# Converting four weight pieces during the first batch of attention, and dividing by the softmax sums with transferred rows on POOL

## The chip, the cores and the metric

The kernel runs on one core of a Trainium2 chip. The metric is the device time of one execution in microseconds (us); the time before is a median of 1040.71 us over three runs (1039.84 to 1042.85). Engines are named as in the profile: PE (matmul, PEld its weight loads), DVE (vector), ACT (scalar), POOL (GpSimd) and SP, whose only work here is to issue transfers.

## The reference

```python
q_bits = (einsum('bhsd,dk->bhsk', q, proj) > 0)          # 6 hash bits, also for k
mask   = bucket(q)[..., :, None] == bucket(k)[..., None, :]
scores = where(mask, q @ k.T / sqrt(64), -1e9)           # B, H, S, D = 4, 8, 768, 64
attn   = exp(scores - max); attn = attn / (attn.sum(-1) + 1e-9)
x      = (attn @ v).transpose(0, 2, 1, 3).reshape(3072, 512)
h      = x @ w_in                                         # 512 x 2048
out    = (h * clip(h + 3, 0, 6) / 6) @ w_out              # 2048 x 512
```

The weights come as 64-bit numbers. Products are made at nearly float32 accuracy: every operand is split into a high part and a low part, and three products (high-high, high-low, low-high) are summed.

## The kernel before

**Attention** is worked off in tiles of 128 keys by all 768 queries, six tiles to a head, eight heads to a batch. The iteration `k` of the main loop makes, in this order: the six transposes of tile k (`transp`, L337), the exponential of tile k+1 (L327, ACT), the minimum of tile k+2 (`lowest`, L315, DVE), half a value product (L374, L375), the split of tile k's transposed probabilities (L360 on ACT, L361 on DVE) and the scores of tile k+3 (L305, L308). Every sixth iteration (k divisible by six) also makes the hash products of the next head but some (`hash_qk`, L265 to L267) and turns them into bits (L276, DVE). POOL prepares queries and keys of a coming head once per head: `scale_q` (L232), the cast and two subtractions of `split_qk` (L253, L257, L258), `split_v` (L291, L292) and two accumulating transfers of outputs (L381). Copies of the cast halves (`kk<-qq`) go by SP's transfers and are needed by the hash products.

Tiles 0 to 47 are batch 0. Iterations 48 to 51 already belong to batch 1; at iteration 51 (`GB` = 52 tiles) attention pauses, and `first_ffn` works off the whole feed-forward part of batch 0: 16 column groups `fc` of the weights by three token chunks, 48 iterations of `gemm1` (L478 to L480), `gate` (L487 to L493) and `gemm2` (L500 to L502). Meanwhile the weights are **converted**: there are 32 pieces (two per `fc`, 128 x 512 each), and `convert` turns a raw 64-bit piece into its high and low part in steps: L175 and L177 on DVE, L182 on ACT, a minimum (L185 on POOL outside the feed-forward part, L188 on DVE inside it), L190 on DVE, L195 on ACT and L196 on POOL. Pieces 0 to 2 are converted beside iterations 45 to 51, the others inside `first_ffn`, a new one begun in two of three iterations (and in all three where `fc` is 4, 6, 8 or 10). Raw pieces and converted ones share one ring of 32 buffers; 28 raw pieces go through it, and the last four use output buffers. After `first_ffn` attention goes on beside the feed-forward part of batches 1 to 3, with all weights converted.

The attention output of batch 0 lies in DRAM undivided (`xs`). Six heads of it (the first three of four 128-row groups) are loaded in three chunks at iterations 40, 41 and 47 and **divided by the sums**: `inverse` (L418, L419), and for each chunk and group `spread` (L426, POOL: each inverse repeated 64 times along the free axis) and `normalise` (two PE transposes L436, then a DVE product L439 with the PSUM result). The first chunk is then split (L469, L470). The last two heads follow as `late`.

**What sets the order:** PE, DVE, ACT and POOL run their instructions in the order in which the code emits them (`manual_schedule`), and each waits in place for what an instruction needs. The table in `early` says which small steps are emitted at the end of which iteration. SP's transfers are put in order by a planner, and SP too waits in place.

Of the kernel before, what the change touches and what calls it, by code (L numbers as in the profile page):

```python
# [10 lines left out]
F32 = mybir.dt.float32  # L11
F32R = mybir.dt.float32r
# [6 lines left out]
P = 128  # L19
# [10 lines left out]
FB = 4  # L30
FS = 4
WL = 28
WE = 8
WA = 3
XE = 8
# [5 lines left out]
def lsh_attention_moe(  # L41
# [101 lines left out]
    def load_w(n: int):  # L143
        fc, k = divmod(n, 2)

        if n < WL:
            raw = cp.tile([P, 2 * WC], F32R, name=f"wr{n}", tag="w", bufs=NW)
        else:
            raw = sp.tile([P, 2 * WC], F32R, name=f"wr{n}", tag="ob")
# [50 lines left out]

    sms = {}


# [342 lines left out]
    room, late, conv, ready, rc0 = {}, {}, {}, {}, []  # L546
    flying = {2: 3}
    cc3 = NCC - 1

    def load0(t: int):  # L550
        xr0[t] = load_x(0, t, range(cc3))

# [19 lines left out]
    def early() -> dict[int, list]:  # L572

        todo = {n: [] for n in range(XE + FB + 1)}

        def put(n: int, *fs):
            todo[n] += fs

        def scaled(t: int):
            def items(x: int):  # L580
                if not sx[t]:
                    if not rc0:
                        rc0.append(inverse("0", 0, slice(0, S), range(cc3)))
                    sx[t].extend(scale_x(0, t, range(cc3), xr0[t], rc0[0][:, 2 * t : 2 * t + 2]))
                sx[t][x]()
            return [lambda x=x: items(x) for x in range(2 + cc3)]

        sx = {t: [] for t in range(NTC)}
        s0, s1, s2 = (scaled(t) for t in range(NTC))
        sp0 = [lambda cc=cc: split_x(x0[0][cc], xr0[0][:, cc], nc.gpsimd) for cc in range(cc3)]  # L590
        c0, c1, c2 = (lambda n=n: cv(n) for n in range(3))
        put(0, lambda: load0(0))
        put(1, lambda: load0(1))
        put(2, s0[0], s0[1], room0)
        put(3, s0[2])
        put(4, s0[3], sp0[0])
        put(5, s0[4], sp0[1], c0)
        put(6, sp0[2], s1[0], s1[1], c0)
        put(7, lambda: load0(2), s1[2], c0, c1)
        put(8, s1[3], c0, c1)  # L600
        put(9, s1[4], c0, c1, s2[0], s2[1], c2)
        put(10, s2[2], c1, c2)
        put(11, s2[3], c1, c2)

        put(12, s2[4])
        return todo
# [3 lines left out]
    def first_ffn(resume):  # L610
# [30 lines left out]
        for n, (fc, t) in enumerate(order):  # L641
# [27 lines left out]
            if n == 0:  # L669
                for f in early_steps[XE + FB]:  # L670
                    f()
# [4 lines left out]
            for x in at:  # L676
                stage[x] += 1
                if stage[x] == 6:
                    del stage[x]
                    if x >= WL and x + 2 < NW:  # L680
                        with tc.issue_after(last.ins):
                            load_w(x + 2)
                        ready[x + 2] = n + 2
            end = finish(*pend) if pend is not None else None
# [155 lines left out]
    with tc.manual_schedule(engines={ET.PE, ET.DVE, ET.Activation, ET.Pool}):  # L840
# [7 lines left out]
        for k in range(NS):  # L848
            end = GB if k < GB else NS
            i, t = divmod(k, KT)  # L850
            if k == HK - XE:
                lent += [cp.tile([P, 2 * WC], F32R, name=f"lent{n}", tag="w", bufs=NW) for n in range(2)]
            if k == GB:
# [40 lines left out]
            if k + LA >= NS:  # L894
                add()
            if HK - XE <= k < GB:
                for f in early_steps[k - HK + XE]:
                    f()
# [71 lines left out]
```

## Time and profile before

| what | value |
|---|---|
| median of three runs | 1040.71 us (1039.84 to 1042.85) |
| the profiled execution's own time | 1040.82 us |
| its span in the profile | 1039.0 us (1.8 us lie around it) |
| mean granted PE clock | 0.994 |
| busy: PE, DVE, ACT, POOL | 1009.5, 687.0, 583.6, 451.4 us |
| batch 0's attention, its last tiles, the first feed-forward part | up to 111, 111 to 147, 147 to about 297 us |

A view by stretches gives, for each stretch of the span, how long each engine was busy and what clock PE was granted. In a timeline a row has start, duration, engine, line, operation, and in brackets how long the engine idled before and what it waited for. In a view by groups a row ends with total busy time, mean duration in ns, and the idle time before the group.

### The profile page before, as it was taken

How to read it: one execution, taken by the hardware profiler on the slowest of the kernel's cores; microseconds unless marked ns; L12 is line 12 of the kernel's file. 1: busy time of each engine (PE TensorE's matmuls, PEld its weight loads, DVE VectorE, ACT ScalarE, POOL GpSimd, SP SyncE). 2: the span in 40 equal slices, each digit the busy share in tenths (PEclk: the TensorE clock that was granted, in tenths of full speed). 3: DMA queues.
4: the chain of work that ended last, by engine and by line, in shares of the span. 5: the costliest groups of instructions: out<-in, count | busy, mean ns of one | idle time of the engine just before them, and what ended most of it. 6: DMA issues, size and time to landing. Idle time of an engine off the chain costs nothing.

```text
span 1039.0 us, 18911 instructions
## 1 busy us (share of the span) xinstructions
PE 1009.5 (97%) x6846; PEld 927.2 (89%) x6846; DVE 687.0 (66%) x1441; ACT 583.6 (56%) x1308; POOL 451.4 (43%) x439
## 2 busy tenths in 40 slices
PE   8999879999999999999999999999999999999998
PEld 7999868887989998899999999999899999899997
DVE  6999888999479998766656666655665563333332
ACT  6888855555478887645554555454455462333332
POOL 5677753334247775645444444544454232200100
PEclk9999989999999999999999999999999999999999
DMA  3666686000144555322222232222232011101000
GB/s 93 155 149 155 187 277 236 1 2 1 46 130 112 120 124 143 80 53 60 75 46 63 61 88 59 53 71 59 60 93 47 15 37 28 42 1 41 1 22 20
DMA packets 47380, 80.68 MB, mean 78 GB/s; under 512 B 5892, under 2 KB 27780, under 8 KB 47288
## 3 DMA queue, kind: packets, MB, share of 16 engines
q1 hardware_dynamic: 42808, 73.98, 24.2%
q0 software_dynamic: 4480, 5.51, 4.6%
q8 instruction: 54, 0.88, 0.4%
q14 instruction: 38, 0.31, 0.1%
HBM read 41.95 MB, written 18.09 MB: 58 GB/s over the span
## 4 chain that ended last, share of the span: by engine, by line
PE 83%; DVE 8%; issue 3%; POOL 2%; ACT 2%; DMA 1%; SPq 0%; DVEq 0%; POOLq 0%; ACTq 0%
PE pt L337 11%; PE h L479 7%; PE h L478 7%; PE h L480 7%; PE po L500 7%; PE po L502 7%; PE po L501 7%; PE acc L374 6%; PE acc L375 6%; PE s L305 6%; PE s L308 6%; DVE wr L175 1%; DVE pl L361 1%; DVE wr L177 1%; PE z L267 1%
## 5 line engine op out<-in xcount | busy, mean ns | idle before, releaser
L315 DVE TENSOR_SCALAR_CACHE_REDUCE p<-s 128x768 f32<-128x768 f32 x192 | 183.5, 956 | 103.5 <-PE pt L337 99.5
L361 DVE TENSOR_TENSOR pl<-pt,ph 128x384 fp32r<-128x384 f32 x376 | 191.8, 551 | 50.4 <-ACT ph L360 48.3
L360 ACT CAST ph<-pt 128x384 fp32r<-128x384 f32 x376 | 165.5, 480 | 57.4 <-PE pt L337 45.0
L327 ACT ACTIVATE p<-p,m 128x768 f32<-128x768 f32 x192 | 179.5, 935 | 5.1 <-DVE p L315 4.8
L487 ACT ACTIVATE g<-h,three 128x256 f32<-128x256 f32 x192 | 91.4, 476 | 155.9 <-PE h L480 141.6
L337 PE MATMUL pt<-ident,p 128*128 128x128 f32 x1152 | 162.2, 275 | 5.9 <-DVE pl L361 4.8
L493 POOL TENSOR_TENSOR gl<-g,gh 128x256 fp32r<-128x256 f32 x96 | 74.2, 773 | 203.7 <-DVE gh L492 160.0
L488 DVE SCALAR_TENSOR_TENSOR g<-g,h 128x256 f32<-128x256 f32 x192 | 80.6, 420 | 117.8 <-ACT g L487 115.3
L337 PEld LDWEIGHTS pt<-ident,p 128*128 128x128 f32 x1152 | 137.3, 141 | 23.6 <-PE pt L337 3.8
L374 PE MATMUL acc<-ph,vv 128*128 128x256 f32 x564 | 152.8, 303 | 1.0 <-DVE pl L361 1.0
L478 PE MATMUL h<-xh,w 128*128 128x256 f32 x512 | 147.7, 289 | 1.2 <-ACT y L402 1.2
L480 PE MATMUL h<-xh,w 128*128 128x256 f32 x512 | 143.4, 280 | 1.3 <-POOL w L196 1.3
L479 PE MATMUL h<-xl,w 128*128 128x256 f32 x512 | 143.2, 280 | 0.6 <-DVE xl L470 0.6
L375 PE MATMUL acc<-pl,vv 128*128 128x256 f32 x564 | 141.1, 283 | 0.0
L500 PE MATMUL po<-w,gh 128*128 128x512 f32 x320 | 126.7, 396 | 1.5 <-ACT gh L492 1.4
L501 PE MATMUL po<-w,gh 128*128 128x512 f32 x320 | 126.2, 394 | 0.9 <-POOL w L196 0.9
L502 PE MATMUL po<-w,gl 128*128 128x512 f32 x320 | 126.6, 396 | 0.0
L374 PEld LDWEIGHTS acc<-ph,vv 128*128 128x128 f32 x564 | 107.5, 191 | 2.2 <-DVE pl L361 1.9
L375 PEld LDWEIGHTS acc<-pl,vv 128*128 128x128 f32 x564 | 107.9, 191 | 0.0
L305 PE MATMUL s<-kk,qq 76*128 76x384 f32 x384 | 101.2, 344 | 2.5 <-ACT kk L281 1.5
L308 PE MATMUL s<-kk,qq 128*128 128x384 f32 x384 | 100.0, 341 | 0.0
L478 PEld LDWEIGHTS h<-xh,w 128*128 128x128 f32 x512 | 96.4, 188 | 3.8 <-ACT y L402 2.4
(134 smaller groups left out, 1999.5 us busy)
## 6 DMA issues: line engine op xcount, KB each, us to landing
raw<-in_qkT SPq DMA_DIRECT2D x32, 384.0 KB, 3.5
kk<-qq SPq DMA_DIRECT2D x62, 192.0 KB, 3.2
wr<-in_w_in SPq DMA_DIRECT2D x16, 512.0 KB, 7.1
wr<-in_w_out SPq DMA_DIRECT2D x16, 512.0 KB, 3.8
vr<-in_v SPq DMA_DIRECT2D x32, 192.0 KB, 2.4
qq<-qq SPq DMA_DIRECT2D x31, 192.0 KB, 3.6
out<-ob SPq DMA_DIRECT2D x11, 512.0 KB, 3.0
xr<-xs SPq DMA_DIRECT2D x9, 512.0 KB
```

The lines of the kernel that those rows point to most:

```text
L315: nc.vector.tensor_scalar(out=pr_[:], in0=s[:, :, :HW], scalar1=CAP, scalar2=None, op0=ALU.min, op1=ALU.min, accum_out=m[:],)
L327: nc.scalar.activation(pr_[:], pr_[:], AF.Exp, bias=m[:], scale=-1.0, accum_out=sms[b][:, t, h : h + 1])
L337: nc.tensor.transpose(pt[:, x], probs[g][0][:, c, x * P : (x + 1) * P], ident[:])
L361: nc.vector.tensor_sub(lo[:, :, w], pt[:], hi[:, :, w].bitcast(F32))
L374: nc.tensor.matmul(acc[:], lhsT=vv[:, kt], rhs=hi[:, x], start=(kt == 0), stop=False)
L375: nc.tensor.matmul(acc[:], lhsT=vv[:, kt], rhs=lo[:, x], start=False, stop=(kt == KT - 1))
L478: nc.tensor.matmul(hp[:], lhsT=wi[:, 0, wc], rhs=xh, start=(cc == 0), stop=False)
L479: nc.tensor.matmul(hp[:], lhsT=wi[:, 0, wc], rhs=xl, start=False, stop=False)
L480: nc.tensor.matmul(hp[:], lhsT=wi[:, 1, wc], rhs=xh, start=False, stop=(cc == NCC - 1))
L500: nc.tensor.matmul(po[u], lhsT=gh[:, us], rhs=wo[:, 0], start=(fc == 0), stop=False)
L501: nc.tensor.matmul(po[u], lhsT=gh[:, us], rhs=wo[:, 1], start=False, stop=False)
L502: nc.tensor.matmul(po[u], lhsT=gl[:, us], rhs=wo[:, 0], start=False, stop=(fc == NFC - 1))
```

## The change

- Pieces 0 to 3 are converted beside iterations 14 to 36 (heads 2 to 6) and get four buffers of their own (`WA` = 4, tag `we`); the other 28 share the ring with 30 raw pieces (`WL` = 30) and six buffers (`lents`) that are taken at the start. Inside `first_ffn` a new piece is begun in three of four iterations.
- The inverse sums of heads 0 to 3 (iteration 25) and of heads 4 and 5 (iteration 37) are turned by six PE transposes into rows, copied by ACT into one buffer, written to DRAM (`rs`) and read back repeated over 64 partitions each (`over`). The first three groups of the output are then multiplied by these rows on POOL (one of nine products on DVE). The nine `spread`, the eighteen transposes L436 and the nine products L439 of these groups go away. The loads move forward (heads 0 to 3 at iterations 30 and 31), and two of three subtractions of the first chunk's split go to DVE (iterations 45, 46).
- The late two heads are divided as before.

```diff
-WL = 28
+WL = 30
-WA = 3
+WA = 4
+WB = 6
...
-        w = wt[n] = cp.tile([P, 2, WC], F32R, name=f"w{n}", tag="w", bufs=NW)
+        w = wt[n] = cp.tile(
+            [P, 2, WC], F32R, name=f"w{n}", tag="we" if n < WA else "w", bufs=WA if n < WA else NW - WA
+        )
...
+    rs = dp.tile([H, S], F32, name="rs", tag="rs", bufs=1)
+    lents = [cp.tile([P, 2 * WC], F32R, name=f"lent{n}", tag="w", bufs=NW - WA) for n in range(WB)]
...
-    flying = {2: 3}
+    flying = {3: 3}
+    rows = lents[0][:, :S].bitcast(F32)
+    over = [x[:, :S].bitcast(F32) for x in lents[1 : 1 + cc3]]
...
+    def divisors(ccs: range):
+        rc0[:] = [inverse("0", 0, slice(0, S), ccs, *rc0)]
+        hs = slice(ccs.start * P // D, ccs.stop * P // D)
+        n = hs.stop - hs.start
+        for j in range(2):
+            rt = bank([P, QT, P], f"rows{hs.start}_{j}")
+            for x in range(QT):
+                nc.tensor.transpose(rt[:n, x], rc0[0][:, j * QT + x, hs], ident[:])
+            nc.scalar.copy(rows[:n, j * HW : (j + 1) * HW], rt[:n].rearrange("h x q -> h (x q)"))
+        dma(out=rs[hs], in_=rows[:n])
+        for cc in ccs:
+            dma(
+                out=over[cc], in_=rs[cc * P // D : (cc + 1) * P // D].unsqueeze(1).to_broadcast([P // D, D, S])
+            )
+
+    def divide(t: int, cc: int, engine):
+        x = xr0[t][:, cc]
+        engine.tensor_mul(x, x, over[cc][:, t * TC : (t + 1) * TC])
...
+        for n, ks in enumerate(((14, 15, 18, 19, 20), (21, 22, 24, 25, 26), (27, 28, 30, 31, 32), (33, 34, 36))):
+            for k in ks:
+                put(k, lambda n=n: cv(n))
+        put(25, lambda: divisors(range(0, 2)))
+        put(30, lambda: load0(0, range(0, 2)))
+        put(31, lambda: load0(1, range(0, 2)))
+        put(37, lambda: divisors(range(2, cc3)))
+        put(38, mul(0, 0), mul(0, 1))
+        put(40, lambda: load0(0, range(2, cc3)))
+        put(41, lambda: load0(1, range(2, cc3)))
+        put(42, room0, mul(1, 0), mul(1, 1))
+        put(44, mul(0, 2), low(0, nc.gpsimd))
+        put(45, low(1, nc.vector))
+        put(46, low(2, nc.vector))
+        put(47, lambda: load0(2, range(cc3)))
+        put(48, mul(1, 2))
+        put(50, mul(2, 0), mul(2, 1))
+        put(GB, mul(2, 2, nc.vector))
...
-            if begun < NW and begun in wraw and (t or n == 0 or begun >= WL or fc in (4, 6, 8, 10)) and n >= ready.get(begun, 0):
+            if begun < NW and n % 4 != 3 and n >= ready.get(begun, 0):
```

In the three pairs below the first block is the kernel before, the second the changed one, whose line numbers are some nine higher.

**DVE at iterations 24 and 25** (L276, later L285, makes the hash bits; L315, later L324, is the minimum; L361, later L370, the split; `wr1` is raw piece 1, `rc0` the inverse sums):

```order
L361 TENSOR_TENSOR pl12_1_1054<-pt24_1_1034,ph12_1_1053 128x3x128
L276 TENSOR_SCALAR qq_5_949<-z5_1059,thr_66,val_67 44x768
L315 TENSOR_SCALAR p27_1083,m27_1082<-s27_1066 128x768
L361 TENSOR_TENSOR pl12_0_1050<-pt25_0_1073,ph12_0_1049 128x3x128
L361 TENSOR_TENSOR pl12_1_1054<-pt25_1_1077,ph12_1_1053 128x3x128
L315 TENSOR_SCALAR p28_1117,m28_1116<-s28_1096 128x768
```

```order
L370 TENSOR_TENSOR pl12_1_1072<-pt24_1_1052,ph12_1_1071 128x3x128
L285 TENSOR_SCALAR qq_5_964<-z5_1077,thr_66,val_67 44x768
L324 TENSOR_SCALAR p27_1103,m27_1102<-s27_1084 128x768
L370 TENSOR_TENSOR pl12_0_1068<-pt25_0_1093,ph12_0_1067 128x3x128
L370 TENSOR_TENSOR pl12_1_1072<-pt25_1_1097,ph12_1_1071 128x3x128
L194 SCALAR_TENSOR_TENSOR wr1_686<-wr1_686 128x512
L427 TENSOR_SCALAR rc0_1126<-sms0_188 128x6x4
L428 RECIPROCAL rc0_1126<-rc0_1126 128x6x4
L324 TENSOR_SCALAR p28_1154,m28_1153<-s28_1116 128x768
```

A conversion step (one of eleven on DVE between iterations 14 and 34) and the two steps of the inverse now stand between one tile's split and the next tile's minimum.

**PE at iteration 25** (`s28` are scores, `pt26` the next tile's transposes, `rows0` the turned inverse sums):

```order
L305 MATMUL s28_1096<-kk_4_735,qq_4_736 128x384 x2
L308 MATMUL s28_1096<-kk_4_735,qq_4_736 128x384 x2
L337 MATMUL pt26_0_1107<-ident_69,p26_1040 128x128 x3
L337 MATMUL pt26_1_1111<-ident_69,p26_1040 128x128 x3
L374 MATMUL acc12_1119<-ph12_0_1049,vv4_1018 128x256
```

```order
L314 MATMUL s28_1116<-kk_4_744,qq_4_745 128x384 x2
L317 MATMUL s28_1116<-kk_4_744,qq_4_745 128x384 x2
L578 MATMUL rows0_0_1129<-ident_69,rc0_1126 4x128 x3
L578 MATMUL rows0_1_1134<-ident_69,rc0_1126 4x128 x3
L346 MATMUL pt26_0_1144<-ident_69,p26_1058 128x128 x3
L346 MATMUL pt26_1_1148<-ident_69,p26_1058 128x128 x3
```

The six transposes of the inverse sums stand ahead of tile 26's, and need DVE's `rc0`, which DVE makes last in the same iteration. The same happens at iteration 37.

**SP before the hash of head 9** (`kk_9`, `qq_9` are the copies that this hash needs, `xr0_2` the third chunk of the output):

```order
L75 DMA kk_9_1825<-qq_9_1826 64x768
L75 DMA qq_9_1826<-qq_9_1826 64x768
L75 DMA kk_9_1825<-qq_9_1826 64x768
L75 DMA xs0_125<-y7_0_1838 64x512
L75 DMA xr0_2_1919<-xs0_125 128x3x256
```

```order
L76 DMA xr0_2_1964<-xs0_125 128x3x256
L76 DMA kk_9_1879<-qq_9_1880 64x768
L76 DMA qq_9_1880<-qq_9_1880 64x768
L76 DMA kk_9_1879<-qq_9_1880 64x768
L76 DMA xs0_125<-y7_0_1892 64x512
```

The load of the third chunk, which needs the buffer of the first chunk (free after iteration 46's subtraction on DVE), now stands ahead of the copies.

More of the change, by code (lines that the diff above doesn't have):

```diff
@@ L146, in load_w @@
         if n < WL:
-            raw = cp.tile([P, 2 * WC], F32R, name=f"wr{n}", tag="w", bufs=NW)
+            raw = cp.tile([P, 2 * WC], F32R, name=f"wr{n}", tag="w", bufs=NW - WA)
         else:
@@ L572, in early, with mul, low @@
     def early() -> dict[int, list]:
-        todo = {n: [] for n in range(XE + FB + 1)}
+        todo = {n: [] for n in range(GB + 1)}
         def put(n: int, *fs):
             todo[n] += fs
[L579 to L605, printed above, removed]
+        def mul(t: int, cc: int, engine=nc.gpsimd):
+            return lambda: divide(t, cc, engine)
+        def low(cc: int, engine):
+            return lambda: split_x(x0[0][cc], xr0[0][:, cc], engine)
+        for n, ks in enumerate(((14, 15, 18, 19, 20), (21, 22, 24, 25, 26), (27, 28, 30, 31, 32), (33, 34, 36))):
[16 more added lines that the diff above has]
+        put(GB, mul(2, 2, nc.vector))
         return todo
@@ L851, in lsh_attention_moe @@
             if k == HK - XE:
-                lent += [cp.tile([P, 2 * WC], F32R, name=f"lent{n}", tag="w", bufs=NW) for n in range(2)]
+                lent += lents[1 + cc3 :]
             if k == GB:
```

20 lines of the change are left out of this document (11 added, 9 removed).

## The prediction

> **What bounds the kernel now.** I read the page's table of engines first, then the view by stretches around batch 0, since every edit lies there.
>
> ```profile
> PE 1009.5 (97%) x6846; PEld 927.2 (89%) x6846; DVE 687.0 (66%) x1441; ACT 583.6 (56%) x1308; POOL 451.4 (43%) x439
> 25.00:95.00 70.00, 70.00 (x525) 68.08 (x524) 64.36 (x130) 60.82 (x139) 50.26 (x41) 1.00 0.64 160
> 110.00:147.30 37.30, 30.53 (x201) 26.71 (x201) 32.41 (x68) 25.63 (x58) 25.78 (x31) 0.91 0.65 191
> 147.30:182.00 34.70, 31.84 (x206) 28.21 (x205) 29.32 (x61) 19.58 (x42) 11.37 (x10) 1.00 0.75 269
> 182.00:257.00 75.00, 71.38 (x435) 60.27 (x435) 70.09 (x126) 42.43 (x88) 29.09 (x20) 1.00 0.00 1
> 257.00:292.00 35.00, 35.00 (x226) 31.83 (x225) 16.99 (x38) 16.43 (x35) 9.21 (x7) 1.00 0.18 49
> ```
>
> The columns are the stretch, its length, the busy time of PE, PEld, DVE, ACT and POOL, PE's granted clock, DMA share and GB/s. PE is 97% busy, so a gain can only come from stretches in which it is not. In the middle of batch 0's attention (25 to 95) PE is never idle, but DVE is 92% busy behind it: this is where the change puts new DVE work. From 110 to 147.3 PE idles 6.8 us (37.30 - 30.53) and has a lower clock: the stretch that the change empties. From 182 to 257 DVE is busy 93% and PE waits for it; from 257, when all weights are converted, PE is full.
>
> Where PE stops in the last tiles of batch 0 (timeline of PE; the first row is tile 42's transposes, the last the first product of the feed-forward part), and what clock it then has:
>
> ```profile
> 111.00 0.82 PE L337 MATMUL pt<-ident,p 128*128 128x128 f32 x6
> ...
> 129.34 0.44 PE L436 MATMUL rt<-ident,rb 128*128 128x128 f32 x2 [1.59 <-POOL rb L426]
> ...
> 137.86 0.52 PE L337 MATMUL pt<-ident,p 128*128 128x128 f32 x3 [2.32 <-DVE pl L361]
> ...
> 140.94 0.69 PE L436 MATMUL rt<-ident,rb 128*128 128x128 f32 x2 [1.66 <-POOL rb L426]
> ...
> 147.29 0.28 PE L478 MATMUL h<-xh,w 128*128 128x256 f32 x1
> ```
>
> ```profile
> 140.00:145.00 5.00, 4.03 (x18) 3.57 (x18) 3.18 (x7) 1.74 (x4) 1.54 (x4) 0.50 0.99 338
> 145.00:150.00 5.00, 5.00 (x40) 4.88 (x39) 3.54 (x9) 3.41 (x10) 3.87 (x4) 0.88 1.06 379
> ```
>
> Two long waits are for a `spread` on POOL, one is for a DVE that also converts; after them PE runs at half clock.
>
> **The end of batch 0 (gain).** The change takes away the transposes L436 of six heads with their waits, the products L439, and the conversions of pieces 0 to 2 from this stretch. The transposes are one group in the view by lines:
>
> ```profile
> L436 PE MATMUL rt<-ident,rb 128*128 128x128 f32 x18 | 4.2, 317 | 3.8 <-POOL rb L426 3.5 <-DVE lent L361 0.2
> ```
>
> Idle 6.8 us; lost to the clock 4.03 x 0.5 = 2.0 and 0.12 x 2.3 = 0.3 us; the transposes half of their 4.2 us, since two records overlap, 2.1 us. That is 11.2 us if nothing takes their place. Two things do. Two subtractions of the first chunk's split come to DVE (iterations 45 and 46); a conversion step twice as wide takes 0.68 us (below), so I count 0.55 us each, 1.1 us. And on SP the copies for the hash of head 9 now stand behind the load of the third chunk, which waits for the second of these subtractions, in iteration 46. The hash is made in iteration 48, two tiles later, 4.5 us at 2.26 us a tile (31 minima in 70 us, below); issuing three transfers takes about 1.5 us and the copy itself
>
> ```profile
> kk<-qq SPq DMA_DIRECT2D x62, 192.0 KB, 3.2
> ```
>
> 3.2 us from issue to landing, so PE waits about 0.2 to 2 us; I take 1.1. Gain: 11.2 - 2.2 = **9.0 us**; between 5.6 (only the three waits quoted, 1.59 + 2.32 + 1.66) and 11.2.
>
> **Conversions beside heads 2 to 6 (loss).** DVE in the steady part, and the same conversion steps where they already stand beside attention tiles (123 to 146):
>
> ```profile
> L315 DVE TENSOR_SCALAR_CACHE_REDUCE p<-s 128x768 f32<-128x768 f32 x31 | 29.7, 958 | 5.3 <-PE pt L337 4.5
> ...
> L175 DVE TENSOR_SCALAR wr<-wr 128x512 uint32<-128x512 uint32 x3 | 2.4, 816 | 0.0
> L177 DVE SCALAR_TENSOR_TENSOR wr<-wr 128x512 uint32<-128x512 uint32 x3 | 2.0, 681 | 0.0
> L190 DVE SCALAR_TENSOR_TENSOR wr<-wr 128x512 uint32<-128x512 uint32 x2 | 1.4, 692 | 0.0
> ```
>
> DVE's only idle time is 5.3 us over 31 tiles, 0.17 us a tile, just before the minimum. Eleven steps come in: four of L175, four of L177, three of L190, 4 x 0.82 + 4 x 0.68 + 3 x 0.69 = 8.1 us. They lie in 23 tiles (14 to 36), which have 23 x 0.17 = 3.9 us. What doesn't fit delays the minimum and the split, for which PE's next transposes wait: **4.2 us** lost. ACT's seven steps are hidden by its 9.2 us of idle time in 70 (70 - 60.82), and cost up to their own duration if that idle time is elsewhere. The price of a DVE step depends on what POOL does at that moment:
>
> ```profile
> 122.21 1.82 POOL L257 TENSOR_TENSOR kk<-raw,qq 64x768 fp32r<-64x768 f32 x1
> ...
> 194.17 1.31 POOL L196 TENSOR_TENSOR w<-wr,w 128x512 fp32r<-128x512 f32 x1 [0.81 <-ACT w L195]
> ...
> 123.55 0.78 DVE L175 TENSOR_SCALAR wr<-wr 128x512 uint32<-128x512 uint32 x1
> ...
> 149.75 0.42 DVE L175 TENSOR_SCALAR wr<-wr 128x512 uint32<-128x512 uint32 x1
> ...
> 194.23 1.80 DVE L177 SCALAR_TENSOR_TENSOR wr<-wr 128x512 uint32<-128x512 uint32 x1
> ```
>
> L175 alone takes 0.42 us; begun during POOL's L257 it ends 0.3 us after that one does (124.33 against 124.03). L177 begun 0.06 us after an L196 takes 1.80 instead of 0.68. So the steps wait out a POOL instruction. What POOL does in the steady part:
>
> ```profile
> L258 POOL TENSOR_TENSOR qq<-raw,qq 64x768 fp32r<-64x768 f32 x6 | 11.1, 1846 | 0.5
> L257 POOL TENSOR_TENSOR kk<-raw,qq 64x768 fp32r<-64x768 f32 x6 | 11.0, 1840 | 0.5
> L232 POOL TENSOR_SCALAR raw<-raw 64x768 f32<-64x768 f32 x5 | 10.8, 2154 | 3.3 <-DMA raw<-in_qkT 2.9 <-DVE qq L276 0.4
> L292 POOL TENSOR_TENSOR vv<-vr,vv 128x384 fp32r<-128x384 f32 x5 | 5.1, 1011 | 0.4
> L253 POOL CAST qq<-raw 128x768 fp32r<-128x768 f32 x5 | 4.1, 822 | 6.0 <-PE s L308 4.8 <-DVE pl L361 1.2
> ```
>
> A step that comes at a random moment finds on average the sum of count x duration squared, over twice 70 us, still to wait: 72.4 / 140 = 0.52 us. The ends: 4 x 0.42 + 7 x 0.68 = 6.4 us without any wait, 2.5 us lost; 6.4 + 11 x 0.52 = 12.1 us at random, 8.2 us lost. I stay with the steps measured beside tiles, whose POOL was as busy (25.78 of 37.30 us, 69%, against 72%).
>
> POOL itself gets eight products of 128 x 256 (at most the 1.01 us of L292) into its 28% idle time. Its chain per head is from L258's end to the next raw operand, and on:
>
> ```profile
> 53.16 1.84 POOL L258 TENSOR_TENSOR qq<-raw,qq 64x768 fp32r<-64x768 f32 x1
> ...
> 60.97 2.14 POOL L232 TENSOR_SCALAR raw<-raw 64x768 f32<-64x768 f32 x1 [1.11 <-DMA raw<-in_qkT]
> ```
>
> 5.97 us to the raw operand, then 2.14 + 0.82 + 1.84 + 1.85, with an L196 of 1.31 between: 13.9 us, against a head of 6 x 2.26 = 13.6 us and 14.7 us with the loss above. It just fits.
>
> The Trainium skill has the rule behind those rows: by "SBUF — State Buffer", section "Who interferes with whom", a vector instruction in its two-port mode or with two SBUF inputs and a GpSimd instruction that reads SBUF exclude each other for the whole instruction. The trace agrees (0.78 and 1.80 us against 0.42 and 0.68), and the rule speaks against this change, since minimum and split take their data from PSUM and the new steps do not; what it makes of the time is the first rival.
>
> **The inverse sums at iterations 25 and 37 (loss).** PE's transposes need DVE's two steps of the same iteration, after the split. At the same place of an earlier head (iterations 13, 14) PE is ready for the next tile while DVE still splits:
>
> ```profile
> 47.73 1.02 DVE L361 TENSOR_TENSOR pl<-pt,ph 128x384 fp32r<-128x384 f32 x2
> ...
> 115.07 0.18 DVE L418 TENSOR_SCALAR rc<-sms 128x36 f32<-128x36 f32 x1
> 115.29 0.38 DVE L419 RECIPROCAL rc<-rc 128x36 f32<-128x36 f32 x1
> ...
> 47.95 0.82 PE L337 MATMUL pt<-ident,p 128*128 128x128 f32 x6
> ```
>
> The split ends at 48.75; 0.18 + 0.38 later, at 49.31, the inverse is there, and PE has waited 1.36 us; its six transposes take about 0.6 us. Iteration 25 is the same with a conversion step ahead, which is counted above. So 2 x 2.0 = **4.0 us**; at least 1.2 (the transposes alone), at most 5.6 if ACT's two copies (at most 0.4 us each on so few partitions) also delay the next exponential. The row transfers run beside tiles and are read 13 tiles (29 us) after iteration 25.
>
> **The feed-forward part of batch 0 (gain).** The first activation of each iteration counts them (same columns by stretch, for L487 alone), and two waits are for the pieces 2 and 3:
>
> ```profile
> 153.50:179.90 26.40, 4.27 (x9) 1.00 0.74 266
> 179.90:255.40 75.50, 11.40 (x24) 1.00 0.00 1
> 257.70:285.60 27.90, 4.75 (x10) 1.00 0.18 43
> ...
> PE h L480 <- POOL w L196: 1.3, 2, 0.7
> PE po L501 <- POOL w L196: 0.9, 1, 0.9
> ```
>
> Without conversion an iteration takes 2.79 us (27.9 / 10); with a new piece in two of three 26.4 / 9 = 2.93, and without the two kinds of wait (2.2 us) no more than 2.79; with five of six 75.5 / 24 = 3.15. Three of four is halfway between two of three and five of six: 2.97. 33 iterations then take 98.0 instead of 101.9 us, 3.9 less; the conversion lasts two iterations longer at 0.18, 0.4. Pieces 0 to 3 are there in time. Gain **3.5 us**; from -2.4 (3.15 throughout: 104.0, and the same 0.4) to 9.8 (2.79 throughout, 92.1).
>
> **Sum.** 9.0 + 3.5 - 4.2 - 4.0 = 4.3 us off the profiled execution's own 1040.82 us (0.1 above the median): **1036.5 us**. The attention of batches 1 to 3 isn't touched.
>
> **Rivals.** *The two engines' lock decides.* Place: heads 2 to 6 and every L196 of the feed-forward part. Price: the steps wait 0.52 us each (8.2 us lost) and three of four costs as much as five of six (2.4 us lost): 9.0 - 2.4 - 8.2 - 4.0 = -5.6, 1046.4 us. For it: L177's 1.80 us, and POOL gets more to do. Against: the eight steps beside tiles. It decides, over 3.1 us slower, when both losses pass 7.9 us, about 0.34 us of wait a step and 3.12 us an iteration. By the page named above this is the normal case.
>
> *The end of batch 0 is held by something else*: the late heads' chain (last value product, output transfer, load) or the hash behind SP. Then only the three waits go: 5.6 + 3.5 - 4.2 - 4.0 = 0.9, 1039.9 us. For it: late heads are divided as before. Against: their chain starts earlier too.
>
> *DVE has room*: 11.2 + 9.8 - 2.5 - 4.0 = 14.5, 1026.3 us; against it stands DVE's 92%.
>
> **How the numbers follow.** Forecast 0.50 (its own range 1032.5 to 1040), the lock 0.24, held end 0.20, room 0.06. No change is within 0.3%, 3.1 us, what a measurement can tell here. Faster: 0.37 of the forecast and the 0.06, 0.43. Slower: 0.22 of the lock and 0.05 of the held end, 0.27. The rest, 0.30, within. The range 1030 to 1046.5 leaves out most of "room" and half of the lock.
>
> **What would show it.** Right: no wait on L426 before the feed-forward part, whose first product comes within 2 us of 147.29 - 9.0 + 4.2 + 4.0 = 146.5; waits of 1.4 to 2 us before the transposes of the sums at iterations 25 and 37; 2.9 to 3.0 us an iteration later. Wrong: conversion steps beside tiles above 1.2 us on average (the lock), a PE wait at the hash of head 9 above 3 us or on the late load (held end), or a POOL chain that makes PE wait for L258's result.

## The result and the profile after

The changed kernel takes 1072.14 us (median of four, 1070.89 to 1073.12), against 1040.87 us of the kernel before on the same chip: ratio 1.0297, 95% interval 1.0278 to 1.0317. The forecast was 1036.5 us in a range of 1030 to 1046.5; it was wrong in sign. The profiled execution has a span of 1069.1 us, 30.1 more than before.

The waits of PE, whole span (engine, line, tile, what it waited for: us in total, times, longest), and PE's rows at the longest of them:

```profile
PE z L275 <- DMA kk<-qq: 22.4, 3, 16.0
PE pt L346 <- DVE pl L370: 6.2, 12, 1.1
PE rows L578 <- DVE rc L428: 4.6, 2, 2.3
```

```profile
79.65 0.82 PE L578 MATMUL rows<-ident,rc 128*4 128x128 f32 x6 [2.32 <-DVE rc L428]
...
106.92 0.62 PE L275 MATMUL z<-kk,pjh 128*108 128x384 f32 x1 [15.98 <-DMA kk<-qq]
...
148.76 0.62 PE L275 MATMUL z<-kk,pjh 128*108 128x384 f32 x1 [5.35 <-DMA kk<-qq]
...
168.13 0.40 PE L275 MATMUL z<-kk,pjh 128*108 128x384 f32 x1 [1.07 <-DMA kk<-qq]
```

A wait that the kernel before did not have stands on top: the hash products at iterations 30 and 42 stand 16 and 5.4 us for the copies `kk<-qq`. What the transfers do meanwhile is in the view by stretches (length, busy PE, PEld, DVE, ACT, POOL, PE's clock, DMA share, GB/s) and in SP's timeline, which gives how long the issue took:

```profile
85.00:86.00 1.00, 1.00 (x11) 0.88 (x9) 1.00 (x4) 1.00 (x3) 0.92 (x2) 1.00 0.11 46
...
86.00:88.00 2.00, 2.00 (x17) 1.88 (x16) 2.00 (x5) 2.00 (x7) 1.93 (x2) 1.00 0.13 52
...
92.00:94.00 2.00, 0.00 (x0) 0.00 (x0) 0.00 (x0) 0.65 (x2) 1.91 (x2) 1.00 1.04 235
...
102.00:104.00 2.00, 0.00 (x0) 0.00 (x0) 0.00 (x0) 0.00 (x0) 0.00 (x0) 0.50 0.13 50
104.00:106.00 2.00, 0.00 (x0) 0.00 (x0) 0.00 (x0) 0.00 (x0) 0.00 (x0) 0.50 0.13 47
```

```profile
83.11 1.15 SPq L76 DMA_DIRECT2D lent<-rs  x2
84.31 5.14 SPq L76 DMA_DIRECT2D wr<-in_w_out  x1
89.50 0.80 SPq L76 DMA_DIRECT2D wr<-in_w_in  x1
90.39 5.58 SPq L76 DMA_DIRECT2D kk<-qq  x1
96.01 0.94 SPq L76 DMA_DIRECT2D qq<-qq  x1
97.00 1.06 SPq L76 DMA_DIRECT2D kk<-qq  x1
```

After the two repeated reads (`lent<-rs`, 384 KB each) the DMA share is 0.11 to 0.13 at 46 to 52 GB/s: 2/16 is 0.125, so two of sixteen engines work. 768 KB at 50 GB/s would take 15.7 us (an estimate from these rows). SP is held up meanwhile (5.14 and 5.58 us for one issue). Once it has issued the weight pieces the share is high (1.04 at 92 to 94), but at the end, 102 to 106, it is again that of two engines, while PE, DVE, ACT and POOL all stand at 0.00 busy and PE waits for the copies. PE's clock has fallen to 0.50 by then.

The Trainium skill states this in "DMA: Bandwidth & Descriptors", section "Why a DMA increments its semaphore by 16 and not by 1": a transfer uses the largest number of engines up to 16 that divides the slowest dimension, larger than one, of both access patterns, and its rules for kernel authors say that an outermost dimension smaller than 16 confines the whole transfer to at most that many engines. The source pattern here is 2 x 64 x 768, with the two heads outermost. The trace agrees (0.13).

**Where the 30.1 us are.** The start of the hash bits (L276 before, L285 after) marks iterations 24, 30, 36 and 42; the first and the last gate of the feed-forward part (L487, L496) mark that. Before, then after:

```profile
72.82 1.09 DVE L276 TENSOR_SCALAR qq<-z,thr,val 44x768 fp32r<-44x768 f32 x1
86.49 1.08 DVE L276 TENSOR_SCALAR qq<-z,thr,val 44x768 fp32r<-44x768 f32 x1
100.16 1.08 DVE L276 TENSOR_SCALAR qq<-z,thr,val 44x768 fp32r<-44x768 f32 x1
113.96 1.09 DVE L276 TENSOR_SCALAR qq<-z,thr,val 44x768 fp32r<-44x768 f32 x1 [0.20 <-PE z L267]
...
148.90 0.48 ACT L487 ACTIVATE g<-h,three 128x256 f32<-128x256 f32 x1
...
292.68 0.47 ACT L487 ACTIVATE g<-h,three 128x256 f32<-128x256 f32 x1 [0.22 <-PE h L480]
```

```profile
74.72 1.09 DVE L285 TENSOR_SCALAR qq<-z,thr,val 44x768 fp32r<-44x768 f32 x1
109.53 1.08 DVE L285 TENSOR_SCALAR qq<-z,thr,val 44x768 fp32r<-44x768 f32 x1 [17.59 <-PE z L276]
126.23 1.08 DVE L285 TENSOR_SCALAR qq<-z,thr,val 44x768 fp32r<-44x768 f32 x1
151.35 1.09 DVE L285 TENSOR_SCALAR qq<-z,thr,val 44x768 fp32r<-44x768 f32 x1 [6.89 <-PE z L276]
...
180.99 0.47 ACT L496 ACTIVATE g<-h,three 128x256 f32<-128x256 f32 x1
...
322.42 0.47 ACT L496 ACTIVATE g<-h,three 128x256 f32<-128x256 f32 x1 [0.22 <-PE h L489]
```

Differences of these rows, of all kernels, from one profiled execution each, in us:

| kernel | 12 to 24 | 24 to 30 | 30 to 36 | 36 to 42 | 42 to first gate | first to last gate | median of the runs |
|---|---|---|---|---|---|---|---|
| before | 27.3 | 13.7 | 13.7 | 13.8 | 34.9 | 143.8 | 1040.7 to 1041.9 |
| after | 29.7 | 34.8 | 16.7 | 25.1 | 29.6 | 141.4 | 1072.1 |
| e7 half the bytes | 29.7 | 29.6 | 16.6 | 20.4 | 29.6 | 141.3 | 1060.9 |
| e1 sixteen engines | 29.7 | 22.7 | 16.1 | 18.3 | 28.2 | 141.4 | 1056.3 |
| e4 + inverse ahead | 29.7 | 22.7 | 16.3 | 17.9 | 28.3 | 141.5 | 1052.1 |
| e5 + copies first | 29.7 | 20.0 | 15.4 | 18.7 | 28.6 | 141.4 | 1048.9 |
| e8 + beside no step | 29.7 | 15.7 | 16.2 | 14.7 | 27.4 | 141.4 | 1040.9 |
| e2 conversions alone | 29.7 | 15.4 | 15.4 | 13.7 | 30.1 | 141.4 | 1041.0 |
| e3 division, late conversions | 27.3 | 21.0 | 15.5 | 17.9 | 35.1 | 141.8 | 1052.2 |
| e6 rate alone | 27.3 | 13.7 | 13.6 | 13.7 | 35.3 | 141.9 | 1039.8 |
| e9 one early piece | 27.3 | 13.9 | 14.1 | 14.7 | 34.9 | 139.7 | 1037.4 |
| e9, again | 27.3 | 13.9 | 14.2 | 13.7 | 34.9 | 139.9 | 1038.7 |
| e10 both | 27.3 | 14.3 | 17.5 | 14.6 | 31.7 | 140.2 | 1040.0 |
| e11 two early pieces | 27.6 | 15.4 | 14.2 | 14.5 | 31.2 | 139.9 | 1037.9 |

After less before: 2.4 + 21.1 + 3.0 + 11.3 - 5.3 - 2.4 = 30.1 us. The two gains are there, and two heads lose over 30 us. The row of e1 is not typical of its kernel: the profiled execution took 1050.69 us and the other three 1056.1 to 1056.9.

### The profile page after: what moved, and what is told of

The parts are those of the page before. It is cut to its first block, busy times and chain, and to the rows that moved or that the text cites. A ratio compares the mean times of both kernels' runs of the same rounds, so it can differ in the third digit from the quotient of the medians.

```text
span 1069.1 us, 18891 instructions
## 1 busy us (share of the span) xinstructions
PE 1014.8 (95%) x6840; PEld 930.8 (87%) x6840; DVE 688.3 (64%) x1436; ACT 583.8 (55%) x1312; POOL 452.1 (42%) x437
## 4 chain that ended last, share of the span: by engine, by line
PE 75%; DVE 10%; issue 5%; ACT 4%; DMA 3%; POOL 2%; SPq 0%; DVEq 0%; POOLq 0%; ACTq 0%
PE pt L346 10%; PE h L488 7%; PE h L487 7%; PE h L489 7%; PE po L509 6%; PE po L511 6%; PE po L510 6%; PE acc L383 5%; PE acc L384 5%; PE s L314 5%; PE s L317 5%; DMA qq<-qq 3%; DVE pl L370 2%; DVE wr L179 2%; DVE p L324 1%
## 5 line engine op out<-in xcount | busy, mean ns | idle before, releaser
L324 DVE TENSOR_SCALAR_CACHE_REDUCE p<-s 128x768 f32<-128x768 f32 x192 | 183.6, 957 | 108.9 <-PE pt L346 104.8
L370 DVE TENSOR_TENSOR pl<-pt,ph 128x384 fp32r<-128x384 f32 x376 | 191.9, 551 | 51.1 <-ACT ph L369 49.1
L369 ACT CAST ph<-pt 128x384 fp32r<-128x384 f32 x376 | 165.4, 480 | 81.7 <-PE pt L346 71.5
L496 ACT ACTIVATE g<-h,three 128x256 f32<-128x256 f32 x192 | 91.3, 475 | 151.3 <-PE h L489 134.0
L346 PE MATMUL pt<-ident,p 128*128 128x128 f32 x1152 | 164.9, 277 | 7.7 <-DVE pl L370 6.2
L346 PEld LDWEIGHTS pt<-ident,p 128*128 128x128 f32 x1152 | 139.5, 143 | 26.6 <-PE pt L346 6.6
L487 PE MATMUL h<-xh,w 128*128 128x256 f32 x512 | 147.7, 289 | 1.2 <-ACT y L411 1.2
L487 PEld LDWEIGHTS h<-xh,w 128*128 128x128 f32 x512 | 96.4, 188 | 3.8 <-ACT y L411 2.4
```

The source lines that it names most:

```text
L324: nc.vector.tensor_scalar(out=pr_[:], in0=s[:, :, :HW], scalar1=CAP, scalar2=None, op0=ALU.min, op1=ALU.min, accum_out=m[:],)
L346: nc.tensor.transpose(pt[:, x], probs[g][0][:, c, x * P : (x + 1) * P], ident[:])
L370: nc.vector.tensor_sub(lo[:, :, w], pt[:], hi[:, :, w].bitcast(F32))
L487: nc.tensor.matmul(hp[:], lhsT=wi[:, 0, wc], rhs=xh, start=(cc == 0), stop=False)
```

## The experiments

**e1: the repeats on sixteen engines.** Two causes could make the copies late: the two engines, or where the repeats stand in SP's order. `D` is 64 and `P // D` is 2.

```diff
-        for cc in ccs:
-            dma(
-                out=over[cc], in_=rs[cc * P // D : (cc + 1) * P // D].unsqueeze(1).to_broadcast([P // D, D, S])
-            )
+        for h in range(hs.start, hs.stop):
+            dma(out=over[h * D // P][h * D % P : h * D % P + D], in_=rs[h : h + 1].to_broadcast([D, S]))
```

> The changed kernel, with each repeated-row transfer (two heads x 64 copies x 768) issued as two transfers of 64 copies x 768; order and place of everything else the same. Theory (few DMA engines): in the changed kernel the DMA share falls to 0.13 (two of sixteen engines) while these transfers run, and the copies for the hash queue behind them on those two engines; with 64 as the outer dimension the three waits of the hash products for kk<-qq (22.4 us) fall below 4 us, PE's half clock after them goes, and the time falls to 1040 to 1046 us. Rival (place in SP's order): the copies are late because they stand behind loads and rows that wait; then the waits stay above 12 us and the time above 1058 us.

Measured: 1056.28 us (1050.69 to 1056.89), ratio 1.0123 (1.0095 to 1.0152); the profiled execution is the fastest of the four. PE's wait at iteration 30, the transfers around it, and SP:

```profile
95.97 0.44 PE L275 MATMUL z<-kk,pjh 128*108 128x384 f32 x1 [4.11 <-DMA kk<-qq]
```

```profile
85.00:87.00 2.00, 2.00 (x17) 1.82 (x16) 2.00 (x6) 2.00 (x7) 1.92 (x3) 1.00 0.76 241
87.00:89.00 2.00, 2.00 (x17) 1.86 (x16) 2.00 (x5) 2.00 (x6) 1.93 (x2) 1.00 0.97 212
...
93.00:95.00 2.00, 0.00 (x0) 0.00 (x0) 0.00 (x0) 0.56 (x2) 1.91 (x2) 1.00 1.02 230
```

```profile
83.85 2.40 SPq L76 DMA_DIRECT2D lent<-rs  x4
86.30 0.59 SPq L76 DMA_DIRECT2D wr<-in_w_out  x1
86.93 0.42 SPq L76 DMA_DIRECT2D wr<-in_w_in  x1
87.45 0.49 SPq L76 DMA_DIRECT2D kk<-qq  x1
```

The same bytes at the same place, but now the DMA share is 0.76 and 0.97 behind their issue, in place of 0.11 to 0.13, so all engines work; the four repeats are issued in 2.40 us and the pieces and copies behind them in 0.4 to 0.8 us each, and the first wait is 4.1 us in place of 16.0. The span of the profiled execution is 20.2 us shorter, the medians differ by 15.9. The time lies between the two expectations: of some 31 us the engines are half by the medians and two thirds by the profiled executions, and not the whole.

**e7: half the bytes on two engines.** A dose for the same claim. This kernel leaves out half of the sums, so its output is not that of the reference; only its time is of use.

```diff
-                out=over[cc], in_=rs[cc * P // D : (cc + 1) * P // D].unsqueeze(1).to_broadcast([P // D, D, S])
+                out=over[cc][:, :HW], in_=rs[cc * P // D : (cc + 1) * P // D, :HW].unsqueeze(1).to_broadcast([P // D, D, HW])
...
-        engine.tensor_mul(x, x, over[cc][:, t * TC : (t + 1) * TC])
+        engine.tensor_mul(x, x, over[cc][:, :TC])
```

> Edit: as the change, with the two-engine repeats, but each repeat moves only the first half of the columns (192 KB in place of 384 KB), and the products take the first 256 columns of it for every chunk of columns, so that the sums of the other rows are left out of the result. Everything else, the place in SP's order and the number of transfers too, is as in the change. Theory that the copies of the next head wait while two engines move the repeats: the wait of PE at the first late hash product is proportional to the bytes, about 8 us in place of 16.0, the second 1-2 us in place of 5.35, and the time is 1057-1062 us in place of 1072. Rival, that the wait belongs to the order of the issues or to the stored row that the repeats read back: the first wait stays above 13 us and the time above 1068 us.

```profile
101.25 0.62 PE L275 MATMUL z<-kk,pjh 128*108 128x384 f32 x1 [8.06 <-DMA kk<-qq]
```

1060.92 us (two runs), as expected: half the bytes, half the wait (8.06 against 15.98), with order and number of transfers unchanged. That the wait is so exactly half is in part luck. After the mark at 24 the copies come 5.2 us earlier (27.0 in place of 32.2 us), and PE comes to its wait 2.7 us later than in the changed kernel: its clock was 0.50 at 80 to 82, and it waited 1.55 us for DVE. Half of 15.7 us would be 7.9. That the copies wait for the two engines' bytes is shown, the exact proportion is not.

**e2: the conversions alone**, with the division of before.

```diff
-        put(25, lambda: divisors(range(0, 2)))
...
+        put(42, s0[0], s0[1], room0)      # spread and normalise, as before
+        put(43, s0[2])
```

> Only the conversions moved (pieces 0 to 3 at iterations 14 to 36, 30 raw pieces in the ring, a new piece in three of four iterations); division by the sums as before, with spread and transposes. If a conversion step beside a tile costs 0.5 us as the trace of the changed kernel shows for the first five (2.5 us), 5.5 us are lost in heads 2 to 6; 2.4 us are gained in the feed-forward part (136.8 against 139.1 us from its second iteration to its last) and 2 to 4 us at the end of batch 0: 1039 to 1042 us. If the lock between DVE and POOL is the main loss of the change: 1046 us or more.

Measured: 1040.99 us, ratio 0.9991 (0.9980 to 1.0002), inside the first expectation, and the lock as the main loss falls. The early conversions cost 5.9 us from 12 to 36, give 4.8 us from 42 to the first gate, and the feed-forward part gives 2.4. Three of the four first steps (L179, which was L175), and the POOL subtraction (L265, which was L257) beside the second of these rows:

```profile
67.77 1.59 DVE L179 TENSOR_SCALAR wr<-wr 128x512 uint32<-128x512 uint32 x1
...
83.13 1.62 DVE L179 TENSOR_SCALAR wr<-wr 128x512 uint32<-128x512 uint32 x1
...
98.55 1.61 DVE L179 TENSOR_SCALAR wr<-wr 128x512 uint32<-128x512 uint32 x1
```

```profile
82.62 1.84 POOL L265 TENSOR_TENSOR kk<-raw,qq 64x768 fp32r<-64x768 f32 x1
```

The eleven steps take 10.4 us here, where the prediction had 8.1: the first of the four L179 takes 0.80 us, the others 1.6, and the steps L181 and L194 stay at 0.68 to 0.69. The three stand at iterations 21, 27 and 33, the same place of three heads, so each begins some 0.5 us after the same subtraction and ends 0.3 us after it (84.75 against 84.46).

**e3: the division on sixteen engines, without early conversions.**

```diff
-        for n, ks in enumerate(((14, 15, 18, 19, 20), (21, 22, 24, 25, 26), (27, ...), (33, 34, 36))):
+        for n, ks in enumerate(((45, 46, 47, 48, 49), (47, 48, 49, 50, 51), (49, 50, 51))):
...
-    flying = {3: 3}
+    flying = {2: 3}
```

> As e1_sixteen, but pieces 0 to 2 are converted beside iterations 45 to 51 as before, and piece 3 in the feed-forward part; the division by transferred rows stays. If conversions beside heads 2 to 6 cost 5.5 us and those beside iterations 45 to 51 some 3 us: 2 to 3 us less than e1_sixteen. If the end of batch 0 needs a free DVE: as much as e1_sixteen or more.

Measured: 1052.22 us, ratio 1.0098 (1.0083 to 1.0113). The heads lose 13.3 us (24 to 42: 54.4 against 41.1) and the end wins nothing (35.1 against 34.9). So most of the loss in the heads comes without early conversions, and with three conversions at 45 to 51 the division gains nothing at the end. Which of the two expectations holds stays open: against e1 the median is 4.1 us less, the profiled execution's span 2.0 us more.

**e4: the inverse one iteration ahead of its transposes.**

```diff
+        put(24, lambda: invert0(range(0, 2)))
         put(25, lambda: divisors(range(0, 2)))     # without the inverse
+        put(36, lambda: invert0(range(2, cc3)))
         put(37, lambda: divisors(range(2, cc3)))
```

> As e1_sixteen, but the two DVE steps of the inverse sums stand one iteration ahead (24 and 36) of the transposes and row copies (25 and 37). PE's two waits for rc (4.6 us in the changed kernel) should go: 2.5 to 4.5 us less than e1_sixteen. If the tile after is held by DVE anyway, less than 1 us.

Measured: 1052.06 us, ratio 1.0089 (1.0072 to 1.0106); span 1048.9 as in e1. The 4.6 us of waits before the turned sums are gone from PE's list, but in the profiled executions 24 to 30 is unchanged (22.7): PE then waits 4.63 us for `kk` at iteration 30, where e1 had 4.11, and 1.57 before a tile's transposes. By these the wait that went has only moved. The medians say otherwise: 4.2 us less than e1, as the theory expected. Since e1's profiled execution is 5.4 to 6.2 us faster than the rest of its runs, the comparison of the profiles can't decide this, and it stays open.

**e5: the next head's copies issued before the repeats.**

```diff
-        put(24, lambda: invert0(range(0, 2)))
-        put(25, lambda: divisors(range(0, 2)))
+        put(27, lambda: invert0(range(0, 2)))
+        put(28, lambda: divisors(range(0, 2)))
...                                              # and 36, 37 become 39, 40
```

> Edit: as e4_inverse_ahead (sixteen-engine repeats, inverse an iteration ahead of its transposes), but the inverse stands at iterations 27 and 39 and the transposes, the row store and the repeats at 28 and 40, so that SP issues the copies of the next head (kk, qq) before the repeats and before the weight pieces that it then lets through. Theory that place in SP's order is what is left of the loss in e4 (its first late hash product still waited 4.6 us for kk, behind some 2 MB): the waits of PE's L275 for kk fall from about 5 us to under 1.5 us in all, the steps 24 to 30 and 36 to 42 fall by 6 to 10 us together, and the time falls from 1052 to 1040-1045 us. Rival, that the repeats cost by their traffic and by the POOL products wherever they stand: the waits move to another tile, and the time stays at 1048 us or above.

Measured: 1048.89 us, ratio 1.0056 (1.0035 to 1.0077). The waits for `kk` fall to 2.0 us in all (6.3 in e4), but 24 to 30 and 36 to 42 only by 1.9 together, and the time is the rival's. What stands in the way now, on DVE and on PE, and PE's clock behind it:

```profile
83.07 1.62 DVE L179 TENSOR_SCALAR wr<-wr 128x512 uint32<-128x512 uint32 x1
84.61 1.77 DVE L427 TENSOR_SCALAR rc<-sms 128x24 f32<-128x24 f32 x1
86.41 0.30 DVE L428 RECIPROCAL rc<-rc 128x24 f32<-128x24 f32 x1
```

```profile
84.47 1.87 POOL L267 TENSOR_TENSOR qq<-raw,qq 64x768 fp32r<-64x768 f32 x1
```

```profile
86.86 0.49 PE L580 MATMUL rows<-ident,rc 128*4 128x128 f32 x3 [2.14 <-DVE rc L428]
...
94.10 0.34 PE L275 MATMUL z<-kk,pjh 128*108 128x384 f32 x1
```

```profile
84.00:86.00 2.00, 0.72 (x5) 0.40 (x3) 2.00 (x2) 0.42 (x1) 1.93 (x2) 1.00 0.88 271
86.00:88.00 2.00, 0.49 (x3) 0.20 (x3) 1.97 (x6) 0.47 (x1) 1.86 (x4) 1.00 0.18 17
...
90.00:92.00 2.00, 2.00 (x10) 2.00 (x10) 1.90 (x4) 1.53 (x5) 0.00 (x0) 0.50 0.01 3
```

The inverse came behind a conversion step, began 0.14 us after a POOL subtraction and ended with it (86.38 against 86.34), at 1.77 us in place of 0.17 (next run). PE stood, and its clock fell to 0.50.

**e8: the inverse beside no conversion step, POOL's products behind its casts.**

```diff
-        put(27, lambda: invert0(range(0, 2)))
-        put(28, lambda: divisors(range(0, 2)))
+        put(29, lambda: invert0(range(0, 2)))
+        put(30, lambda: divisors(range(0, 2)))
...                                              # the loads of 30 and 31 go to 32 and 33
-        put(38, mul(0, 0), mul(0, 1))
-        put(42, room0, mul(1, 0), mul(1, 1))
-        put(44, mul(0, 2), low(0, nc.gpsimd))
+        put(40, ..., mul(0, 0), mul(0, 1))        # inverse of heads 4, 5 at 40, rows at 41
+        put(46, mul(0, 2), low(0, nc.gpsimd))
+        put(47, mul(1, 0), mul(1, 1))
```

> Edit: as e5_copies_first, but the inverse of heads 0 to 3 stands at iteration 29, which has no conversion step, with the rows at 30, behind the next head's copies; that of heads 4 and 5 at 40 with the rows at 41, and the products on POOL that stood at 38, 42 and 44 now at 40, 46 and 47, behind POOL's casts of the next head. In e5 the first inverse waited behind a conversion step of 1.62 us and took 1.77 us itself, PE stood 2.1 us and its clock fell to 0.5; at 38 two products of POOL stood ahead of the next head's cast. Theory that what e5 still lost to the division (4.6 us from 24 to 30, 5.0 us from 36 to 42 against e2) is these two collisions: 24 to 30 falls to 16-17 us, 36 to 42 to 14-16 us, PE's first wait for rc to under 0.5 us, and the time to 1041-1044 us. Rival, that the division by rows costs its own work (transposes, traffic of 1.2 MB, nine products) wherever it stands: the two stretches sum to over 36 us and the time stays at 1046 us or above.

```profile
88.05 0.17 DVE L427 TENSOR_SCALAR rc<-sms 128x24 f32<-128x24 f32 x1
...
88.46 0.90 DVE L324 TENSOR_SCALAR_CACHE_REDUCE p<-s 128x768 f32<-128x768 f32 x1
```

```profile
90.36 0.82 PE L580 MATMUL rows<-ident,rc 128*4 128x128 f32 x6
```

Measured: 1040.93 us (1037.86 to 1041.32), ratio 0.9989 (0.9979 to 1.0000). The transposes wait for nothing, and no hash product waits for `kk`. The whole change, its transfers and its products included, now costs no more than e2. The rival (it costs its own work wherever it stands) falls: against e2 the division costs 2.1 us from 24 to 42 and gains 2.7 from there to the first gate. The edit also moves two loads. Neither these nor the products were moved apart from the inverse, so which of the moves is worth what is not shown.

**e6: the rate alone** (thirty raw pieces, a new piece in three of four iterations; conversions at 45 to 51 and division as before).

```diff
-            if begun < NW and begun in wraw and (t or n == 0 or ...) and n >= ready.get(begun, 0):
+            if begun < NW and n % 4 != 3 and n >= ready.get(begun, 0):
```

> Edit: of the change only the 30 raw pieces, the ring that they are read through, and the rule that begins a piece in three iterations of four; the conversions of pieces 0 to 2 stay at iterations 45 to 51, piece 3 is converted in the feed-forward part, and the division is the one of before. Theory that the feed-forward gain belongs to the rule and that everything else of the change loses or breaks even: first to last gate 141.4-141.8 us against 143.8 before, the steps of the heads as before, time 1038.3-1039.3 us, faster than before by 0.2%. Rival, that the regular 3.0 us of an iteration needs the fourth converted piece at the start: first to last gate stays at 143-144 us and the time within 1 us of before.

Measured: 1039.80 us, eleven runs, ratio 0.9983 (0.9974 to 0.9992). First to last gate 141.9 in place of 143.8: the rule is worth 1.9 us by itself. The median is 0.5 us above the expectation.

**e9: e6 with one early piece**, run twice.

```diff
-        for n, ks in enumerate((..., (49, 50, 51))):
+        for n, ks in enumerate((..., (27, 28, 30, 31, 32))):
...
-    flying = {2: 3}
+    flying = {}
```

> Edit: e6_rate_alone with only piece 2 converted early (steps at iterations 27, 28, 30, 31, 32 in place of 49 to 51 and three in the feed-forward part); the other conversions and the division as before. Theory that an early conversion earns about what it costs: the stretch 24 to 30 to 36 grows by 1.5-1.8 us (as in e2 for a piece), the first gate comes 1-2.5 us sooner after iteration 48, and the time is 1038.5-1040.5 us, the same as e6. Rival, that only the steps of the last iterations before the feed-forward part cost anything there: the first gate comes 3 us or more sooner after iteration 48 and the time is 1037.5 us or less, faster than e6 and before.

> The kernel of e9_one_early_piece once more, since its profiled span (1037.7 us) was no shorter than e6's (1037.4) while its median was 2.4 us lower. If e9 is faster than e6: median 1036.5-1038.5 us, ratio to before 0.996 again. If the first five times fell low by chance: median 1039-1040 us, ratio 0.998-0.999.

Measured: 1037.38 us, ratio 0.9960 (0.9947 to 0.9973), and again 1038.73 us, ratio 0.9963 (0.9950 to 0.9977): faster than before. The second median lies between its two expectations, its ratio is the first one's. Against e6 (0.9983) it is some 0.2% less, at the edge of what these intervals separate. Neither theory had the place: the first gate does not come sooner (42 to first gate 34.9), the first feed-forward iterations are shorter (rows of the second time):

```profile
149.95 0.47 ACT L495 ACTIVATE g<-h,three 128x256 f32<-128x256 f32 x1
153.48 0.47 ACT L495 ACTIVATE g<-h,three 128x256 f32<-128x256 f32 x1
155.49 0.48 ACT L495 ACTIVATE g<-h,three 128x256 f32<-128x256 f32 x1
```

5.54 us for the first two, 7.15 in e6 and 7.17 before. The three kernels in which no piece is half converted when the feed-forward part begins (e9, e10, e11: 5.5 to 6.0) have this, the others not; which step of such a piece costs the 1.6 us was not tried.

**e11: two early pieces; e10: e9 with the division placed as in e8.**

```diff
-        (45, 46, 47, 48, 49), (47, 48, 49, 50, 51), (27, 28, 30, 31, 32)     # e9
+        (45, 46, 47, 48, 49), (21, 22, 24, 25, 26), (27, 28, 30, 31, 32)     # e11
```

> Edit: e9_one_early_piece with piece 1 also converted early (iterations 21, 22, 24, 25, 26 in place of 47 to 51). Theory that each early piece earns about what it costs: the heads grow by 1.5-1.8 us once more, the first gate comes 1-2 us sooner after iteration 48, the time stays within 1 us of e9 (1037-1039 us). Rival, that what remains at iterations 45 to 51 is what holds the end: time at 1035.5 us or less.

> Edit: e9_one_early_piece with the division by rows as placed in e8_beside_no_step. In e8 the division cost 2.1 us in the heads against e2 (46.6 us from 24 to 42 in place of 44.5) and won 2.7 us between iteration 42 and the first gate (27.4 in place of 30.1). Theory that these add to e9's: 1036-1038 us, the same as e9 within 0.15%. Rival, that the division wins nothing while conversions stand at iterations 45 to 51 (in e3 the stretch from 42 to the first gate was 35.1 us, as in the kernel before): 42 to the first gate stays at 34-35 us, and the time is 1038.5-1041 us.

e11: 1037.86 us, ratio 0.9955 (0.9937 to 0.9973), as e9: against the two profiled executions of e9 the second piece costs 1.6 and 2.6 us from 12 to 42 and gives 3.7 before the first gate, which the medians do not show. e10: 1040.01 us, ratio 0.9981 (0.9968 to 0.9995), some 0.2% more than e9, again at the edge of what the intervals separate. The time is the rival's, but not by its mechanism: the division does win at the end, beside two conversions (31.7 in place of 34.9), and the heads lose more, 46.3 us from 24 to 42 against 42.7 and 41.7; 1.5 us of it is a wait for `kk` at iteration 36, which e8 does not have.

## Why the prediction was wrong

**The step that failed** is one sentence of the part on the inverse sums: "The row transfers run beside tiles and are read 13 tiles (29 us) after iteration 25." It costed three transfers at nothing because their reader comes late. Their reader was not the point. It left out what is queued behind them: the next head's copies, which stand after them on SP and which PE wanted at 90.9 (106.92 - 15.98), 8 us after the repeats were issued (83.11). The runs showed in its place a wait of 16.0 us at iteration 30 and of 5.4 at 42, and e1 and e7 that the two engines make the larger part of the first. The prediction looked for exactly such a queue in one place (head 9, behind the third load) and not in the other two, and none of its signs of being wrong looks there either. The size was open to it as well: the diff shows the pattern of 2 x 64 rows. The Trainium skill says in the section cited above how many engines such a pattern gets. By the prediction's own row for 145 to 150 (share 1.06 at 379 GB/s), two of sixteen move 45 GB/s, so 768 KB would have been priced at some 17.5 us of transfer (an estimate), twice the 8 us until PE wants the copies.

**The other terms, taken one by one, held in sign.** They can be read in e8, where the transfers and the inverse are out of the way, and in e2:

- End of batch 0: gain 9.0 forecast; 7.5 in e8 (34.9 - 27.4), inside the given 5.6 to 11.2. In the changed kernel itself 5.3. The wait for the copies of head 9 was forecast at 1.1 us and is 1.07, behind the third load as forecast; that it is so near is luck, given 0.2 to 2. In e8 SP issues these copies ahead of that load, and the wait is gone. No transposes of six heads wait before the feed-forward part.
- Conversions beside heads 2 to 6: loss 4.2 forecast; 5.9 in e2, inside 2.5 to 8.2. The steps took 10.4 us there and not 8.1, and 4.5 of them were hidden, not 3.9: what was mis-sized is the price of L179. A step took 0.95 us on average, not the 1.2 that was named as the sign of the lock. Without any wait they would take 6.4 us, so a step waited 0.36 us, which lies between the forecast's 0.15 and the rival's 0.52. Neither a random moment nor the average of steps elsewhere describes it: the schedule repeats with every head, and one kind of step met the same POOL instruction three times.
- Inverse sums: loss 4.0 forecast, for the transposes and their waits. The waits are 2.32 and 2.29 us (1.4 to 2 forecast), and the six transposes take 0.82 us, not 0.6. The two copies on ACT, bounded at 0.4 us each because of their few partitions, take 0.46 to 0.47 us on 4 and on 2 partitions, as much as L369 does on 128 (0.48). In e8 all of the division costs 2.1 us in the heads.
- Feed-forward part: gain 3.5 forecast; 2.4. 1.9 of it belongs to the rate (e6).

With these sizes the sum is 7.5 + 2.4 - 5.9 - 2.1 = 1.9 us of gain, and e8's span is 2.0 us shorter than before. That the two agree confirms nothing, since the sizes are read from the same spans. The runs put the gain at 0 to 2.2 us (ratio 0.9979 to 1.0000). The rest, from the changed kernel to e8, is place: 20.2 us for the two engines (after to e1) and 11.9 for what stands in whose queue (e1 to e8) by the spans, 15.9 and 15.4 by the medians. What stood in a queue were copies behind repeats and weights and the inverse behind a conversion step on DVE; for the products ahead of the next head's cast on POOL it is argued, not shown.

**The rivals.** The three looked at engines and at the end of the batch; none had the repeats as the mechanism. "The hash behind SP" came nearest in place but at head 9 alone. The lock that the slow rival built on does occur (1.77 us in place of 0.17 in e5, 1.6 in place of 0.42 in e2). In e5 PE waited for the locked step at once and stood 2.14 us; in e2 it was part of a loss of 5.9 us, and the change without the division came out even. The rival's threshold is off by a little: by its own terms the losses would have to pass 9.0 - 4.0 + 3.1 = 8.1 us, not 7.9.

## What to carry to other kernels

A transfer that is read late is not free: ask which transfers stand behind it, when those are needed, and on how many engines it runs. The number of engines can be read from the access pattern before a run, and from the DMA share after it: 0.13 is two of sixteen. A waiting time that repeats with the schedule is not an average: look which instruction stands beside the new one in each round. And a small instruction for which PE waits (here an inverse of 0.17 us) should not be put behind a long one for which nothing waits, nor beside a POOL instruction that it has to wait out: the steps from e1 to e8 move instructions and transfers only and are worth 11.9 us by the spans and 15.4 by the medians, more than any saving of work in this change.

## What was not expected of the hardware

A transfer on few engines can also hold the issuing queue: behind 768 KB on two engines SP needed 5.14 and 5.58 us to issue the first weight piece and the first copy, behind half of it (e7) 1.33 and 1.81, and on sixteen engines (e1) 0.59 and 0.49. Behind the single repeat of heads 4 and 5 (384 KB, issued at 133.81) the next issues took 0.42 to 0.60 us. That PE's clock falls was in the prediction for the end of batch 0; not expected was how little is enough: in e5 PE was busy 1.21 of 4 us (84 to 88), and at 90 to 92 had 0.50. Nor does the same wait always do it: before the turned sums PE stood 2.32 us in the changed kernel and kept 1.00 (78 to 84), and stood 2.35 us in e7 and had 0.50 (80 to 82). In the changed kernel its first hash product after the wait takes 0.62 us (106.92), in e5, at full clock again, 0.34 (94.10), so a wait also costs behind its end.
